# Folds of pairs 1 to 3 on GpSimd alone, and the softmax steps around the experts' first layer put in another order

## The chip, the cores and the metric

One core of a Trainium2 chip, with its engines PE (TensorE), DVE (VectorE), ACT (ScalarE), POOL (GpSimd), SP (SyncE, which only issues DMAs here) and 16 DMA engines. The metric is the device time of one execution in microseconds; several executions are timed, and one more is taken with the hardware profiler.

## The reference

All data are float32. `x` is 8 sequences of 2496 tokens with 256 features.

```python
X = np.fft.fft(np.fft.fft(x, axis=1), axis=2).real      # [8, 2496, 256]
x = X.reshape(19968, 256)
logits = x @ phi                                        # 32 slots = 8 experts x 4
d = softmax(logits, axis=0)                             # over the tokens
slot_input = (d.T @ x).reshape(8, 4, 256)
slot_out[e] = relu(slot_input[e] @ w1[e]) @ w2[e]       # 256 -> 1024 -> 256
out = softmax(logits, axis=1) @ slot_out                # over the slots
```

(Both softmaxes subtract their maximum and add 1e-9 to the sum.)

## The kernel before

The host reorders `x` so that a sequence of 2496 tokens becomes 64 by 39, and the eight sequences become four pairs. The transform is never written out: the logits come from small transforms of `x` times transformed `phi`, and `d.T @ x` is taken on the untransformed side and transformed afterwards. For each pair `p` the kernel loads four pieces `t` of 128x1280 as two DMAs each, `x` and its mirror `xm` (640 KB each, 20.97 MB in all), and then runs these parts, named by one letter in the string `ORDER` (`f13` is part `f` of pair 1, piece 3):

- `f` (line 247) adds `xm` onto `x` in place: the fold. `FOLDV` names the folds on DVE (00 to 03, 13, 23); the others are GpSimd's. A tile of `xm` has five buffers, so the load of a later piece waits for a fold.
- `a` (L253) transposes the folded piece on DVE; `z` (L267) multiplies it with the transformed `phi` on PE into four PSUM banks; `t` (L286) transposes these on DVE. For pair 1, `z12` and `z13` need only pieces 2 and 3; for pair 2 each `z` needs all four pieces.
- `b` (L295) and `c` (L309) finish the logits on PE, ACT copies them out, `n` (L317) takes their maxima on DVE and so frees the banks that the next `z` writes; `i`, `j` turn the maxima round and take the exponential on ACT.
- `e` (L349) and `d` (L367) transform the exponentials back, `u` (L393) multiplies them with the folded `x`: the pair's sum in PSUM. ACT copies the first three pairs' sums to `usb`. `tok` holds the sum of the exponentials.
- `m0` (L430 to L439) rescales between the pairs, `m1` (L442 to L449) adds up `usb` into `acc` and makes the reciprocal from `tok`, `m2` (L451 to L464) adds the last pair's sum and transforms `acc` with small matmuls (accT, slotin) into `sT`.
- `k` issues the loads of the experts' weights into freed buffers. `l` (L475 to L482) is the first layer: 64 matmuls `h`, in two halves of two quarters each; ACT applies the relu to each quarter and DVE transposes it into `hT`. `v` (L490) is the second layer `so`, `r` (L501 to L506) brings its result into `rh`.
- `s`, `S`, `x`, `y`, `g`, `q` are the softmax over the slots, for each pair `p`: transposes of the logits on PE (L517), copies on ACT (L529), and for the two pieces 0 and 1 the maximum on DVE (L538), subtraction on GpSimd (L539), exponential on ACT (L544), sum and reciprocal on DVE (L549 to L551), multiplication on GpSimd (L552) and transposition on DVE (L558).
- `o` (L578, L583, L587) multiplies that with `rh` on PE; ACT and DVE take turns in copying out, and SP issues 23 output DMAs of 20.45 MB in all.
- `W` (L278) is a matmul whose result is not used.

Each engine runs its instructions strictly in the order in which they appear: `in_order` chains each engine's instructions in the order of `LD` (first loads) and `ORDER`. An instruction that waits holds up all that stand behind it on its engine. Loads are issued on SP's queue where the `f` of their piece stands, if `LD` has not issued them.

Of the kernel before, what the change touches and what calls it, by code (L numbers as in the profile page):

```python
# [7 lines left out]
AF = mybir.ActivationFunctionType  # L8
ALU = mybir.AluOpType
# [7 lines left out]
NSLOT = 32  # L17
# [13 lines left out]
LD = "00 0 1 p 01 02 03 2 10 11 3 12 13".split()  # L31

ORDER = (
# [9 lines left out]
).split()  # L43
# [97 lines left out]
def _build(nc, tc, xh, phih, wh, cins, where, out):  # L141
    from contextlib import ExitStack

    v, sc, pe, gp = nc.vector, nc.scalar, nc.tensor, nc.gpsimd
    ctx = ExitStack()
    with ctx:
# [14 lines left out]
        def tagged(shape, name, tag, bufs):  # L161
            return sb.tile(shape, F32, name=name, tag=tag, bufs=bufs)
# [9 lines left out]
        def bank(name):  # L172
            return pp.tile([128, 512], F32, name=name, tag="ps")
# [4 lines left out]
        eo, xm, xT, zb, zt, o1, dpm, esb, dsb = {}, {}, {}, {}, {}, {}, {}, {}, {}  # L178
# [65 lines left out]
        def part_f(p, t):  # L244
            if (p, t) not in eo:
                load_x(p, t)
            (v if f"{p}{t}" in FOLDV else gp).tensor_tensor(eo[p, t], eo[p, t], xm[p, t], op=ALU.add)  # L247

        def part_a(p, t):
            ah, h = t % 2, t // 2  # L250
# [151 lines left out]
        w1t, w2t = [], []  # L402
# [18 lines left out]
        sm = cp.tile([128, 40], F32, name="sm")  # L421
# [5 lines left out]
        def part_m(step):  # L427
            if step == 0:
                ps = bank("msel")
                pe.matmul(  # L430
                    ps[:, : NPAIR * GS], C("sel"), mall.rearrange("p a s -> p (a s)"), start=True, stop=True
                )
                v.tensor_tensor(
                    mm, ps[:, : NPAIR * GS].rearrange("p (a s) -> p a s", s=GS),
                    C("mask").unsqueeze(1).to_broadcast([128, NPAIR, GS]), op=ALU.mult,
                )
                v.tensor_reduce(sm[:, 0:4], mm, axis=AX.X, op=ALU.add)
                v.tensor_reduce(sm[:, 4:5], sm[:, 0:4], axis=AX.X, op=ALU.max, negate=True)
                sc.activation(sm[:, 8:12], sm[:, 0:4], AF.Exp, bias=sm[:, 4:5], scale=1.0)  # L439
                return  # L440
            if step == 1:
                v.tensor_scalar(acc, usb[:, 0], sm[:, 8:9], None, op0=ALU.mult)  # L442
                for p in range(1, NPAIR - 1):
                    v.scalar_tensor_tensor(acc, usb[:, p], sm[:, 8 + p : 9 + p], acc, op0=ALU.mult, op1=ALU.add)
                v.tensor_tensor(sm[:, 12:16], sm[:, 8:12], tok, op=ALU.mult)
                v.tensor_reduce(sm[:, 5:6], sm[:, 12:16], axis=AX.X, op=ALU.add)
                v.tensor_scalar(sm[:, 6:7], sm[:, 5:6], 1e-9, None, op0=ALU.add)
                v.reciprocal(sm[:, 7:8], sm[:, 6:7])
                v.tensor_scalar(sm[:, 16:18], C("mask8"), sm[:, 7:8], None, op0=ALU.mult)  # L449
                return  # L450
            v.scalar_tensor_tensor(acc, ubs[-1][:, :D], sm[:, 11:12], acc, op0=ALU.mult, op1=ALU.add)  # L451
            ps = bank("accT")
            pe.matmul(ps[:, 0:64], acc[:, 0:128], C("psum"), start=True, stop=False)
            pe.matmul(ps[:, 0:64], acc[:, 128:256], C("pdif"), start=False, stop=True)
            pe.matmul(ps[:1, 64:96], acc[:, 0:1], C("psum")[:, 0:32], start=True, stop=False)
            pe.matmul(ps[:1, 64:96], acc[:, 128:129], C("pneg"), start=False, stop=True)
            v.tensor_copy(at[:, :64], ps[:, :64])
            v.tensor_copy(at[:1, 32:64], ps[:1, 64:96])
            for lc in range(2):
                ps = bank3(f"slotin{lc}")  # L460
                ls = slice(lc * 128, lc * 128 + 128)
                pe.matmul(ps[:, :NSLOT], C("ta")[:, ls], at[:, 0:32], start=True, stop=False)
                pe.matmul(ps[:, :NSLOT], C("tb")[:, ls], at[:, 32:64], start=False, stop=True)
                (sc.copy, v.tensor_copy)[lc](sT[:, lc], ps[:, :NSLOT])  # L464
# [2 lines left out]
        rh = []  # L467
        sos_ = []

        def part_l(eh):  # L470
            for fh in range(2):
                ps = bank(f"h{eh}{fh}")
                for lc in range(2):
                    for g in range(4):
                        pe.matmul(  # L475
                            ps[32 * g : 32 * g + 32, :], sT[:, lc, :], w1t[16 * eh + 8 * fh + 4 * lc + g],
                            start=lc == 0, stop=lc == 1, tile_position=(0, 32 * g),
                        )
                hs = tagged([128, 512], f"hs{eh}{fh}", "dpm", 2)
                sc.activation(hs, ps, AF.Relu, scale=sm[:, 16 + eh : 17 + eh])  # L480
                hT[eh, fh] = tagged([128, 16, NSLOT], f"hT{eh}{fh}", "hT", 3)
                v.transpose(hT[eh, fh].rearrange("p f s -> p (f s)"), hs)  # L482

        def part_v(eh):
            if eh == 0:
                sos_.append(pu.tile([128, 512], F32, name="so", tag="u"))
            so = sos_[0]
            for f in range(8):
                for g in range(4):
                    pe.matmul(  # L490
                        so[32 * g : 32 * g + 32, 0:D], hT[eh, f // 4][:, 4 * (f % 4) + g, :],
                        w2t[32 * eh + 4 * f + g],
                        start=eh == 0 and f == 0, stop=eh == 1 and f == 7, tile_position=(0, 32 * g),
                    )
# [102 lines left out]
        def in_order(f, *a):  # L597
# [15 lines left out]
            "f": part_f, "a": part_a, "w": lambda *_: part_w(), "z": part_z, "t": lambda p, _: part_t(p),  # L613
            "b": lambda p, _: part_b(p), "c": part_c, "n": lambda p, _: part_n(p), "i": lambda p, _: part_i(p), "j": lambda p, _: part_j(p),
            "e": part_e, "d": lambda p, _: part_d(p), "u": part_u, "k": lambda i, _: load_w(i),
            "m": lambda i, _: part_m(i), "l": lambda i, _: part_l(i), "v": lambda i, _: part_v(i),
            "r": lambda *_: part_r(), "s": part_s, "S": part_S, "W": part_warm, "x": part_x, "y": part_y, "g": part_g, "q": part_q, "o": part_o,
        }
        for what in LD:
# [59 lines left out]
```

## Time and profile before

| | |
|---|---|
| median of 3 runs | 203.81 us (203.43 to 205.42) |
| the profiled execution's own time | 204.89 us |
| its span, first to last instruction | 202.7 us |
| busy: PE, DVE, ACT, POOL | 158.3, 109.2, 78.5, 50.2 us |
| read and written by DMA | 38.84 MB, 20.45 MB |

The busy shares are means over stages with different limits: loading until about 57 us, dense matmuls until about 121, a chain of small steps until 148.5, output until the end. So the views used below are those in order of time, engine by engine. All times of the trace count from the span's start.

### The profile page before, as it was taken

What the parts mean: (1) busy time and instruction counts of PE and PEld (TensorE: products, weight loads), DVE (VectorE), ACT (ScalarE), POOL (GpSimd) and SP (SyncE); (2) the same over time, 40 slices, a digit from 0 to 9 for tenths busy, and PEclk for the clock granted to TensorE, in tenths of its full rate; (3) what the DMA queues carried; (4) which work ended last, traced back from release to release, by engine and by line L of the source; (5) the groups of instructions that cost most, each with busy time, mean ns of one, the idle gap of its engine ahead of it and who ended that gap; (6) DMA issues with size and microseconds to landing.
All of it is one profiled execution on the core that took longest, in us unless ns stands there. A gap on an engine that the chain in (4) does not pass through costs nothing.

```text
span 202.7 us, 5655 instructions
## 1 busy us (share of the span) xinstructions
PE 158.3 (78%) x2500; PEld 98.3 (48%) x2500; DVE 109.2 (54%) x168; ACT 78.5 (39%) x176; POOL 50.2 (25%) x30
## 2 busy tenths in 40 slices
PE   0496799639989999999999893999889897785000
PEld 0454564339734576457747672624446353563000
DVE  0689286564971592251131076428657999997000
ACT  2001023421650635563647641333048776646000
POOL 0000593999920000000000052314200634400000
PEclk9999999966996999999999997579999999769655
DMA  6999999999910079829967938000019999999995
GB/s 211 401 421 411 405 410 411 415 409 413 413 57 0 5 279 406 348 52 421 428 284 283 384 122 323 7 3 0 3 66 395 415 427 412 420 425 415 423 419 223
DMA packets 11544, 59.65 MB, mean 294 GB/s; under 512 B 1536, under 2 KB 1792, under 8 KB 8448
## 3 DMA queue, kind: packets, MB, share of 16 engines
q1 hardware_dynamic: 11520, 59.29, 72.9%
q8 instruction: 19, 0.31, 0.6%
q14 instruction: 5, 0.04, 0.1%
HBM read 38.84 MB, written 20.45 MB: 292 GB/s over the span
## 4 chain that ended last, share of the span: by engine, by line
PE 41%; DMA 24%; DVE 16%; POOL 5%; issue 3%; ACT 2%; SPq 0%; DVEq 0%; POOLq 0%
DMA xm<-xh 24%; PE u L393 6%; DVE o L583 6%; PE z L267 6%; PE po L578 6%; PE e L349 4%; PE d L367 3%; POOL x L247 3%; PE h L475 3%; PE a L295 3%; PE l L309 3%; DVE cm L549 2%; PE cT L517 2%; POOL c L539 2%; DVE cm L538 2%
## 5 line engine op out<-in xcount | busy, mean ns | idle before, releaser
L247 POOL TENSOR_TENSOR x<-x,xm 128x1280 f32<-128x1280 f32 x10 | 29.8, 2997 | 26.6 <-DMA xm<-xh 26.6
L267 PE MATMUL z<-xT,wz 32*64 32x160 f32 (+1 forms) x768 | 27.6, 388 | 8.3 <-DVE zt L283 6.0
L578 PE MATMUL po<-ct,rh 32*128 32x512 f32 (+1 forms) x192 | 30.1, 615 | 4.3 <-DVE ct L558 1.9
L539 POOL TENSOR_TENSOR c<-c,cm 128x512 f32<-128x512 f32 (+1 forms) x8 | 10.1, 1269 | 84.5 <-DVE cm L538 84.5
L583 DVE COPY o<-po 128x512 f32<-128x512 f32 (+1 forms) x40 | 24.5, 661 | 3.3 <-PE po L578 3.3
L267 PEld LDWEIGHTS z<-xT,wz 32*64 32x64 f32 x768 | 17.5, 148 | 17.0 <-DVE xT L253 6.6
L583 ACT COPY o<-po 128x512 f32<-128x512 f32 (+1 forms) x40 | 21.3, 578 | 9.3 <-PE po L578 8.5
L253 DVE STREAM_TRANSPOSE xT<-x 128x1280 f32<-128x1280 f32 x16 | 23.4, 1492 | 1.8 <-POOL x L247 1.6
L578 PEld LDWEIGHTS po<-ct,rh 32*128 32x128 f32 x192 | 16.8, 205 | 13.4 <-DVE o L583 8.3
L338 ACT ACTIVATE d<-lt,nm 120x128 f32<-120x128 f32 x44 | 13.3, 388 | 19.0 <-DVE zt L283 11.5
L393 PE MATMUL u<-x,ds 128*32 128x256 f32 x320 | 18.6, 380 | 0.0
L286 DVE STREAM_TRANSPOSE zt<-z 128x320 f32<-128x320 f32 x16 | 11.3, 839 | 10.6 <-PE z L267 10.6
L247 DVE TENSOR_TENSOR x<-x,xm 128x1280 f32<-128x1280 f32 x6 | 11.6, 1927 | 9.4 <-DMA xm<-xh 9.4
L552 POOL TENSOR_TENSOR c<-c,cm 128x512 f32<-128x512 f32 (+1 forms) x8 | 10.1, 1263 | 16.2 <-DVE cm L551 12.7
L317 DVE TENSOR_REDUCE mx<-l 120x4 f32<-120x512 f32 (+1 forms) x12 | 7.1, 633 | 12.7 <-ACT lt L312 12.7
L393 PEld LDWEIGHTS u<-x,ds 128*32 128x32 f32 x320 | 11.4, 110 | 4.9 <-issue 0.2
L300 ACT COPY o<-a 128x512 f32<-128x512 f32 (+1 forms) x12 | 6.6, 551 | 17.1 <-PE a L295 16.7
L295 PEld LDWEIGHTS a<-cs,zt 128*64 128x64 f32 x352 | 10.9, 138 | 2.3 <-DVE zt L286 1.0
L295 PE MATMUL a<-cs,zt 128*64 128x64 f32 x352 | 11.7, 223 | 0.3 <-issue 0.2
L349 PE MATMUL e<-cs,d 120*64 120x60 f32 x352 | 11.5, 225 | 0.3 <-issue 0.3
L349 PEld LDWEIGHTS e<-cs,d 120*64 120x64 f32 x352 | 10.9, 140 | 1.0 <-issue 0.8
L355 ACT COPY e<-e 128x480 f32<-128x480 f32 (+1 forms) x12 | 6.4, 530 | 12.5 <-PE e L349 12.1
(87 smaller groups left out, 165.8 us busy)
## 6 DMA issues: line engine op xcount, KB each, us to landing
out<-o SPq DMA_DIRECT2D x15, 1024.0 KB, 9.1
w<-wh SPq DMA_DIRECT2D x9, 1280.0 KB, 7.3
x<-xh SPq DMA_DIRECT2D x16, 640.0 KB, 11.2
xm<-xh SPq DMA_DIRECT2D x16, 640.0 KB, 10.6
out<-o SPq DMA_DIRECT2D x4, 896.0 KB, 10.3
w<-wh SPq DMA_DIRECT2D x5, 512.0 KB, 10.5
out<-o SPq DMA_DIRECT2D x4, 256.0 KB, 3.1
w<-wh SPq DMA_DIRECT2D x1, 896.0 KB, 7.4
```

The lines of the kernel that those rows point to most:

```text
L247: (v if f"{p}{t}" in FOLDV else gp).tensor_tensor(eo[p, t], eo[p, t], xm[p, t], op=ALU.add)
L253: v.transpose(xT[p, ah][:, XW * h : XW * h + XW], eo[p, t])
L267: pe.matmul(zb[p][i][64 * ah : 64 * ah + 64, 160 * h0 : 160 * (h0 + n)], wz[r, j % 4, j // 4, :], xv[r, :, j, :], start=j == 0, stop=j == ...
L286: v.transpose(o[:, :, NQ * i : NQ * i + NQ], zb[p][i][:, :320].rearrange("p (h q s) -> p h q s", h=2, s=32))
L295: pe.matmul(ps[64 * r : 64 * r + 64, 64 * i : 64 * i + 64], zt[p][:, o : o + 64], C("wa")[:, 64 * r : 64 * r + 64], start=True, stop=True, ...
L338: sc.activation(d[:, g], lt[p][:, g0 + g], AF.Exp, bias=nm[:, g0 + g : g0 + g + 1], scale=1.0)
L349: pe.matmul(o[64 * k : 64 * k + 64, :, h, g], dd[p, b][:, g, 64 * h : 64 * h + 64], C("ec")[:, 60 * k : 60 * k + 60].rearrange("p (c x) -> ...
L393: pe.matmul(ub[32 * g : 32 * g + 32, 0:D], dsb[p][:, k, h, ah, q, :], eo[p, 2 * h + ah][:, D * q : D * q + D], start=cc == 0, stop=cc == 9 ...
L539: gp.tensor_tensor(c, c, m[:, 0].unsqueeze(2).to_broadcast([128, n, NSLOT]), op=ALU.subtract)
L552: gp.tensor_tensor(c, c, m[:, 1].unsqueeze(2).to_broadcast([128, n, NSLOT]), op=ALU.mult)
L578: pe.matmul(po[:, j * w : j * w + w], rh[0][rows, 128 * dc : 128 * dc + 128], t[rows, r0 * NSLOT : r0 * NSLOT + w], start=True, stop=True, ...
L583: (v.tensor_copy if n_ev[0] % 2 else sc.copy)(ot[:, o : o + w * len(dcs)], po[:, : w * len(dcs)])
```

## The change

Folds 13 and 23 go to GpSimd, and `f13` and `f23` stand in `ORDER` with the others of their pairs, which also moves their loads. The matmul `W31` goes; `a23` stands behind `n10`. `m1` is cut in two: `m1` (the sums over `usb`) stands right behind `m0`, `m2` (from `tok` to the reciprocal) before pair 0's softmax, and what was `m2` is `m3`. `l` is issued by quarters, with `hT` in four buffers, and the softmax steps of pairs 0 and 1 stand between them in another order.

```diff
--- before.py
+++ after.py
@@ -23,7 +23,6 @@
 ZW = 664
 RING, NXM, NET = 8, 5, 2
 
-FOLDV = ("00", "01", "02", "03", "13", "23")
 APART = (0, 1)
 KP = ((0, 16), (16, 24))
 CT = ["sa", "lt", "lt", "lt"]
@@ -31,13 +30,13 @@
 LD = "00 0 1 p 01 02 03 2 10 11 3 12 13".split()
 
 ORDER = (
-    "f00 a00 w00 f01 a01 z00 z01 f02 a02 f03 a03 z02 z03 W23 f10 f11 f12 f20 f21 f22 f30 f31 f32 f33 "
-    "t00 a10 a11 b00 c00 c01 a12 c02 n00 z10 z11 i00 j00 W31 f13 a13 z12 z13 "
-    "e00 e01 e02 t10 b10 a20 a21 d00 a22 c10 c11 c12 f23 a23 n10 "
+    "f00 a00 w00 f01 a01 z00 z01 f02 a02 f03 a03 z02 z03 W23 f10 f11 f12 f13 f20 f21 f22 f23 f30 f31 f32 f33 "
+    "t00 a10 a11 b00 c00 c01 a12 c02 n00 z10 z11 i00 j00 a13 z12 z13 "
+    "e00 e01 e02 t10 b10 a20 a21 d00 a22 c10 c11 c12 n10 a23 "
     "z20 z21 i10 z22 j10 z23 t20 u00 u01 k00 k10 b20 a30 a31 a32 a33 e10 e11 e12 c20 c21 c22 n20 d10 "
     "z30 z31 i20 z32 j20 z33 k20 t30 u10 u11 k30 b30 k40 e20 e21 e22 c30 c31 c32 n30 d20 "
-    "i30 u20 j30 u21 k50 m00 s00 s01 s02 e30 e31 e32 k60 d30 S00 S01 S02 x00 x01 y00 y01 u30 m10 g00 u31 s10 m20 k70 s11 s12 "
-    "S10 S11 S12 g01 x10 l00 q00 x11 y10 y11 q01 g10 g11 l10 q10 q11 v00 v10 r00 "
+    "i30 u20 j30 u21 k50 m00 m10 s00 s01 s02 e30 e31 e32 k60 d30 u30 m20 S00 S01 S02 x00 x01 y00 u31 s10 m30 k70 s11 s12 "
+    "y01 g00 g01 S10 S11 S12 x10 x11 l00 l01 y10 q00 q01 l10 y11 g10 l11 g11 v00 q10 q11 v10 r00 "
     "o00 s20 S20 o01 s21 S21 o02 s22 S22 o03 x20 x21 o04 y20 o10 y21 g20 o11 g21 s30 S30 o12 q20 s31 S31 o13 s32 S32 x30 o14 q21 x31 "
     "o20 y30 o21 y31 g30 o22 g31 o23 q30 o24 q31 o30 o31 o32 o33 o34"
 ).split()
@@ -244,7 +243,7 @@
         def part_f(p, t):
             if (p, t) not in eo:
                 load_x(p, t)
-            (v if f"{p}{t}" in FOLDV else gp).tensor_tensor(eo[p, t], eo[p, t], xm[p, t], op=ALU.add)
+            (v if p == 0 else gp).tensor_tensor(eo[p, t], eo[p, t], xm[p, t], op=ALU.add)
 
         def part_a(p, t):
             ah, h = t % 2, t // 2
@@ -442,6 +441,8 @@
                 v.tensor_scalar(acc, usb[:, 0], sm[:, 8:9], None, op0=ALU.mult)
                 for p in range(1, NPAIR - 1):
                     v.scalar_tensor_tensor(acc, usb[:, p], sm[:, 8 + p : 9 + p], acc, op0=ALU.mult, op1=ALU.add)
+                return
+            if step == 2:
                 v.tensor_tensor(sm[:, 12:16], sm[:, 8:12], tok, op=ALU.mult)
                 v.tensor_reduce(sm[:, 5:6], sm[:, 12:16], axis=AX.X, op=ALU.add)
                 v.tensor_scalar(sm[:, 6:7], sm[:, 5:6], 1e-9, None, op0=ALU.add)
@@ -467,19 +468,18 @@
         rh = []
         sos_ = []
 
-        def part_l(eh):
-            for fh in range(2):
-                ps = bank(f"h{eh}{fh}")
-                for lc in range(2):
-                    for g in range(4):
-                        pe.matmul(
-                            ps[32 * g : 32 * g + 32, :], sT[:, lc, :], w1t[16 * eh + 8 * fh + 4 * lc + g],
-                            start=lc == 0, stop=lc == 1, tile_position=(0, 32 * g),
-                        )
-                hs = tagged([128, 512], f"hs{eh}{fh}", "dpm", 2)
-                sc.activation(hs, ps, AF.Relu, scale=sm[:, 16 + eh : 17 + eh])
-                hT[eh, fh] = tagged([128, 16, NSLOT], f"hT{eh}{fh}", "hT", 3)
-                v.transpose(hT[eh, fh].rearrange("p f s -> p (f s)"), hs)
+        def part_l(eh, fh):
+            ps = bank(f"h{eh}{fh}")
+            for lc in range(2):
+                for g in range(4):
+                    pe.matmul(
+                        ps[32 * g : 32 * g + 32, :], sT[:, lc, :], w1t[16 * eh + 8 * fh + 4 * lc + g],
+                        start=lc == 0, stop=lc == 1, tile_position=(0, 32 * g),
+                    )
+            hs = tagged([128, 512], f"hs{eh}{fh}", "dpm", 2)
+            sc.activation(hs, ps, AF.Relu, scale=sm[:, 16 + eh : 17 + eh])
+            hT[eh, fh] = tagged([128, 16, NSLOT], f"hT{eh}{fh}", "hT", 4)
+            v.transpose(hT[eh, fh].rearrange("p f s -> p (f s)"), hs)
 
         def part_v(eh):
             if eh == 0:
@@ -613,7 +613,7 @@
             "f": part_f, "a": part_a, "w": lambda *_: part_w(), "z": part_z, "t": lambda p, _: part_t(p),
             "b": lambda p, _: part_b(p), "c": part_c, "n": lambda p, _: part_n(p), "i": lambda p, _: part_i(p), "j": lambda p, _: part_j(p),
             "e": part_e, "d": lambda p, _: part_d(p), "u": part_u, "k": lambda i, _: load_w(i),
-            "m": lambda i, _: part_m(i), "l": lambda i, _: part_l(i), "v": lambda i, _: part_v(i),
+            "m": lambda i, _: part_m(i), "l": part_l, "v": lambda i, _: part_v(i),
             "r": lambda *_: part_r(), "s": part_s, "S": part_S, "W": part_warm, "x": part_x, "y": part_y, "g": part_g, "q": part_q, "o": part_o,
         }
         for what in LD:
```

GpSimd's queue of folds before (`x_0_99`, `x_1_103` are pair 1's `x`, `x_0_288`, `x_1_293` pair 2's, the number behind `xm_` is the piece, the last row is of pair 3):

```order
L247 TENSOR_TENSOR x_0_99<-x_0_99,xm_2_108 128x1280 [waits DMAHW2_49,DMAHW1_49]
L247 TENSOR_TENSOR x_0_288<-x_0_288,xm_0_289 128x1280 [waits DMAHW6_49,DMAHW5_49]
L247 TENSOR_TENSOR x_1_293<-x_1_293,xm_1_294 128x1280 [waits DMAHW7_49,DMAHW0_49]
L247 TENSOR_TENSOR x_0_288<-x_0_288,xm_2_298 128x1280 [waits DMAHW2_49,DMAHW1_49]
L247 TENSOR_TENSOR x_0_302<-x_0_302,xm_0_303 128x1280 [waits DMAHW4_49,DMAHW3_49]
```

and with the change (`x_0_289`, `x_1_294` are now pair 2's):

```order
L246 TENSOR_TENSOR x_0_99<-x_0_99,xm_2_108 128x1280 [waits DMAHW2_49,DMAHW1_49]
L246 TENSOR_TENSOR x_1_103<-x_1_103,xm_3_111 128x1280 [waits DMAHW4_49,DMAHW3_49]
L246 TENSOR_TENSOR x_0_289<-x_0_289,xm_0_290 128x1280 [waits DMAHW6_49,DMAHW5_49]
L246 TENSOR_TENSOR x_1_294<-x_1_294,xm_1_295 128x1280 [waits DMAHW7_49,DMAHW0_49]
L246 TENSOR_TENSOR x_0_289<-x_0_289,xm_2_299 128x1280 [waits DMAHW2_49,DMAHW1_49]
L246 TENSOR_TENSOR x_1_294<-x_1_294,xm_3_303 128x1280 [waits DMAHW4_49,DMAHW3_49]
```

Fold 13 stands between 12 and 20, fold 23 between 22 and 30; the loads moved with fold 23, so that the last piece to come in is 33 instead of 23.

DVE's queue before, from pair 2's transposes to its maxima (`xT` is the transposed piece, `mx` the maxima of pair 1's logits):

```order
L253 STREAM_TRANSPOSE xT_0_662<-x_0_288 128x1280 [waits Pool_49]
L247 TENSOR_TENSOR x_1_293<-x_1_293,xm_3_702 128x1280 [waits DMAHW4_49,DMAHW3_49]
L253 STREAM_TRANSPOSE xT_1_664<-x_1_293 128x1280 [waits DVE_49]
L317 TENSOR_REDUCE mx_707<-l_0_693 120x4 [waits Activation_49]
L317 TENSOR_REDUCE mx_707<-l_1_696 120x4 [waits Activation_49]
L317 TENSOR_REDUCE mx_707<-l_2_699 120x3 [waits Activation_49]
```

and with the change:

```order
L252 STREAM_TRANSPOSE xT_0_664<-x_0_289 128x1280 [waits Pool_49]
L316 TENSOR_REDUCE mx_704<-l_0_695 120x4 [waits Activation_49]
L316 TENSOR_REDUCE mx_704<-l_1_698 120x4 [waits Activation_49]
L316 TENSOR_REDUCE mx_704<-l_2_701 120x3 [waits Activation_49]
L252 STREAM_TRANSPOSE xT_1_666<-x_1_294 128x1280 [waits Pool_49]
```

The fold has left the queue, and the last transpose stands behind the maxima.

DVE's queue before, between pair 0's softmax maxima (`cm`) and the last pair's sum (`u`):

```order
L538 TENSOR_REDUCE cm_1_1508<-c_1405 128x24
L442 TENSOR_SCALAR acc<-usb,sm 128x256
L444 SCALAR_TENSOR_TENSOR acc<-usb,sm,acc 128x256 [waits DVE_49] x2
L445 TENSOR_TENSOR sm<-sm,tok 128x4 [waits Activation_49]
L446 TENSOR_REDUCE sm<-sm 128x1 [waits DVE_49]
L447 TENSOR_SCALAR sm<-sm 128x1 [waits DVE_49]
L448 RECIPROCAL sm<-sm 128x1 [waits DVE_49]
L449 TENSOR_SCALAR sm<-cs_70,sm 128x2 [waits DVE_49]
L549 TENSOR_REDUCE cm_0_1505<-c_1405 128x16
L550 TENSOR_SCALAR cm_0_1505<-cm_0_1505 128x16 [waits DVE_49]
L551 RECIPROCAL cm_0_1505<-cm_0_1505 128x16 [waits DVE_49]
L451 SCALAR_TENSOR_TENSOR acc<-u_1523,sm,acc 128x256 [waits PE_49]
```

and with the change:

```order
L450 TENSOR_SCALAR sm<-cs_70,sm 128x2 [waits DVE_49]
L538 TENSOR_REDUCE cm_0_1542<-c_1406 128x16 [waits Activation_49]
L538 TENSOR_REDUCE cm_1_1545<-c_1406 128x24
L452 SCALAR_TENSOR_TENSOR acc<-u_1513,sm,acc 128x256 [waits PE_49]
L458 COPY at<-accT 128x64 [waits PE_49]
L459 COPY at<-accT 1x32 [waits DVE_49]
L465 COPY sT<-slotin_1587 128x32 [waits PE_49]
L549 TENSOR_REDUCE cm_0_1542<-c_1406 128x16 [waits Activation_49]
```

Only the two maxima stand between the small steps on `sm` and the last pair's sum; the softmax's sums and reciprocals come behind the copy of `sT`.

## Rows read from the trace of the kernel before

**Rows 1.** The page's second part, the span in 40 slices of 5.07 us: TensorE's granted clock in tenths, and what the DMA engines moved.

```profile
PEclk9999999966996999999999997579999999769655
...
GB/s 211 401 421 411 405 410 411 415 409 413 413 57 0 5 279 406 348 52 421 428 284 283 384 122 323 7 3 0 3 66 395 415 427 412 420 425 415 423 419 223
```

**Rows 2.** The chain that ended last, in order of time, between 28 and 59 us: start us, us, what.

```profile
28.41 12.79 DMA xm<-xh
...
47.99 8.99 DMA xm<-xh
...
57.08 1.50 DVE x L247
```

**Rows 3.** SyncE's queue in order of time, from 126 us on: start us, us, engine, line, operation.

```profile
150.32 36.82 SPq L587 DMA_DIRECT2D out<-o  x23
```

**Rows 4.** DVE in order of time, 36 to 62 us: start us, us, engine, line, operation, in brackets the idle time before and what ended it.

```profile
38.17 0.17 DVE L334 COPY nm<-mt 120x11 f32<-120x11 f32 x1 [0.32 <-PE mt L332]
...
38.26 4.10 DVE L247 TENSOR_TENSOR x<-x,xm 128x1280 f32<-128x1280 f32 x1
...
42.40 1.51 DVE L253 STREAM_TRANSPOSE xT<-x 128x1280 f32<-128x1280 f32 x1
...
48.52 2.83 DVE L286 STREAM_TRANSPOSE zt<-z 128x320 f32<-128x320 f32 x4 [4.55 <-PE z L267]
...
60.04 1.72 DVE L317 TENSOR_REDUCE mx<-l 120x4 f32<-120x512 f32 x3
```

**Rows 5.** The view of line 247 (the fold), its GpSimd and its DVE instructions: count, shortest/median/longest ns, first and last start, form.

```profile
L247 POOL TENSOR_TENSOR x<-x,xm x10: 2883/2914/3782, 20.9 to 54.0; 128x1280 f32<-128x1280 f32 x10
...
L247 DVE TENSOR_TENSOR x<-x,xm x6: 1491/1493/4102, 6.7 to 57.1; 128x1280 f32<-128x1280 f32 x6
```

**Rows 6.** PE in order of time, 22 to 88 us, columns as in Rows 4.

```profile
22.94 1.33 PE L267 MATMUL z<-xT,wz 32*64 32x160 f32 x60 [1.27 <-issue]
...
38.06 1.13 PE L278 MATMUL warm<-cs,cs 128*128 128x512 f32 x2
...
43.96 4.54 PE L267 MATMUL z<-xT,wz 32*64 32x160 f32 x120 [4.34 <-DVE zt L283]
...
51.41 0.33 PE L295 MATMUL a<-cs,zt 128*64 128x64 f32 x2
...
56.85 2.62 PE L309 MATMUL l<-o,cs 128*120 128x512 f32 x6
...
83.84 2.41 PE L267 MATMUL z<-xT,wz 32*64 32x320 f32 x64
```

**Rows 7.** Busy time of each engine in stretches of the front: us, busy us and instructions of PE, PE's weight loads, DVE, ACT, POOL, then the granted clock, the DMA share and GB/s.

```profile
40.00:44.00 4.00, 0.04 (x6) 0.04 (x6) 3.94 (x3) 1.76 (x7) 3.68 (x2) 0.76 1.01 408
...
44.00:48.50 4.50, 4.50 (x122) 4.04 (x123) 0.00 (x0) 0.00 (x0) 4.50 (x3) 0.50 1.02 415
...
48.50:51.50 3.00, 3.00 (x90) 2.89 (x91) 2.98 (x5) 1.15 (x3) 3.00 (x2) 0.93 1.01 407
...
60.00:65.00 5.00, 4.41 (x63) 2.37 (x62) 1.75 (x4) 0.00 (x0) 0.00 (x0) 0.76 0.01 2
```

**Rows 8.** GpSimd in order of time, 20 to 62 us, columns as in Rows 4.

```profile
28.48 2.91 POOL L247 TENSOR_TENSOR x<-x,xm 128x1280 f32<-128x1280 f32 x1 [0.37 <-DMA xm<-xh]
...
34.86 2.89 POOL L247 TENSOR_TENSOR x<-x,xm 128x1280 f32<-128x1280 f32 x1 [3.47 <-DMA xm<-xh]
...
41.33 12.39 POOL L247 TENSOR_TENSOR x<-x,xm 128x1280 f32<-128x1280 f32 x4 [0.32 <-DMA xm<-xh]
...
53.97 2.94 POOL L247 TENSOR_TENSOR x<-x,xm 128x1280 f32<-128x1280 f32 x1 [0.25 <-DMA xm<-xh]
```

**Rows 9.** One later pair's row maxima: DVE, then the matmuls of PE that they follow, 99 to 103 us, columns as in Rows 4.

```profile
101.55 1.16 DVE L317 TENSOR_REDUCE mx<-l 120x4 f32<-120x512 f32 x2 [0.17 <-ACT lt L312]
...
99.44 2.10 PE L309 MATMUL l<-o,cs 128*120 128x512 f32 x5
```

**Rows 10.** PE in order of time, 116 to 149 us, columns as in Rows 4.

```profile
116.11 4.82 PE L393 MATMUL u<-x,ds 128*32 128x256 f32 x79
...
124.80 0.66 PE L453 MATMUL accT<-cs,acc 128*128 128x64 f32 x2 [3.31 <-DVE acc L451]
...
129.80 9.27 PE L475 MATMUL h<-w,sT 128*32 128x512 f32 x64
...
143.17 3.66 PE L490 MATMUL so<-w,hT 128*32 128x256 f32 x64 [0.65 <-DVE hT L482]
...
148.55 1.14 PE L578 MATMUL po<-ct,rh 32*128 32x512 f32 x8 [0.52 <-DVE rh L506]
```

**Rows 11.** DVE in order of time, 119 to 125 us, columns as in Rows 4.

```profile
119.99 2.10 DVE L444 SCALAR_TENSOR_TENSOR acc<-usb,sm,acc 128x256 f32<-128x256 f32 x2
...
122.25 0.17 DVE L445 TENSOR_TENSOR sm<-sm,tok 128x4 f32<-128x4 f32 x1 [0.15 <-ACT tok L386]
...
124.26 0.39 DVE L451 SCALAR_TENSOR_TENSOR acc<-u,sm,acc 128x256 f32<-128x256 f32 x1
```

**Rows 12.** GpSimd in order of time at the same place, columns as in Rows 4.

```profile
118.76 2.54 POOL L539 TENSOR_TENSOR c<-c,cm 128x512 f32<-128x512 f32 x2 [61.85 <-DVE cm L538]
```

**Rows 13.** The first layer of the experts in two stretches, columns as in Rows 7.

```profile
129.87:134.20 4.33, 4.33 (x24) 1.05 (x28) 0.87 (x2) 1.11 (x2) 2.48 (x2) 0.50 0.01 4
...
134.70:139.00 4.30, 4.30 (x48) 1.21 (x44) 2.81 (x5) 1.21 (x2) 0.35 (x1) 1.00 0.00 0
```


## The prediction

> **What bounds the kernel now.** I read the slices first, to see where DMA is the limit and where not. It moves over 400 GB/s in slices 2 to 11 (5 to 56 us) and again from slice 31 on; between, most of all from 127 to 147 us, it moves next to nothing [rows 1]. So loading and storing are two stretches of fixed length, and what lies between decides. The last piece of `x` lands at 47.99 + 8.99 = 56.98 us, and the chain runs through these loads into a fold on DVE [rows 2]. The first output is issued at 150.32 [rows 3] and DMA is full from then to the end of the span, so the end follows the first output at a fixed distance: 202.7 less the start of `po` at 148.55 [rows 10] is 54.2 us. Everything gained ahead of `po` is gained at the end.
>
> In the middle I then read each engine in order of time and look for holes of PE. **Front:** PE stands idle 4.34 us ahead of 43.96 [rows 6], because fold 13 on DVE takes 4.10 us (38.26 to 42.36) [rows 4] where the median DVE fold takes 1.49 [rows 5]; its transpose ends at 43.91. The granted clock then is 0.50 (1.2 of 2.4 GHz) from 44 to 48.5 [rows 7], so 120 `z` matmuls take 4.54 us [rows 6] instead of 2 x 1.33 = 2.66, at the full rate of the 60 at 22.94 [rows 6]. A second hole follows `c12`, which ends at 56.85 + 2.62 = 59.47 [rows 6]: `z20` writes into banks that pair 1's maxima free, and these, behind fold 23 and its transpose, end at 60.04 + 1.72 = 61.76 [rows 4]. From there to the end of `u31` at 116.11 + 4.82 = 120.93 [rows 10] PE has no such hole. **Tail:** accT starts at 124.80 after 3.31 us of idle [rows 10], since the last sum on DVE starts only at 124.26, behind steps that wait for `tok` until 122.25 [rows 11]. After that hole the clock is at 0.50 as far as 134.20 [rows 13].
>
> **Front, with the change.** GpSimd gets two folds more: 12 x 2.91 = 35.0 us [rows 5]. A piece of `x` is 1.31 MB, 3.19 us at 411 GB/s [rows 1]; twelve are 38.3 us, so GpSimd keeps up. Fold 13 falls into the 3.47 us that GpSimd now idles ahead of 34.86 [rows 8] and is over by about 34.5. Loads wait for folds no later than before. Fold 23 takes the place of the second of the four folds from 41.33 [rows 8] and ends near 47.5; fold 33 becomes the last, 57 to 60 us, and pair 3's `z` starts only at 83.84 [rows 6], so I cost it at nothing.
>
> On DVE the transpose `a13` follows the copy that ends at 38.34 [rows 4]: 38.35 to 39.87 with 1.51 us [rows 4]. The rest of `z12`, `z13` runs from 39.9 for 2.6 us to 42.5 (before: 48.50): 4.1 us from the fold, 1.9 from the clock. The warm matmul of 1.13 us [rows 6] goes, which costs nothing as PE waits there. `t10` takes 2.83 us [rows 4], to 45.4; `b10` started then too (51.35, 51.41), and from there to the end of `c12` took 59.47 - 51.41 = 8.06 [rows 4, 6]: now 53.5. The maxima of a pair end 102.71 - 101.54 = 1.17 us after its last `l` matmul [rows 9], at 54.7, and `a23`, now behind them, adds 1.51: `z20` runs on at 56.2, against 61.76. **Front: 5.6 us.** What is late next is that wait of 2.7 us, 0.4 longer than before; I let the clock fall there as it did (0.76 on the mean from 60 to 65) [rows 7].
>
> Ends: if the clock falls already at `z12`, the 1.9 and some 0.4 in `e` are lost: 3.3. If it doesn't fall at `z20` either, the 62 matmuls there gain 2.4 more by the 64 at 83.84 [rows 6]: 8.0.
>
> **Tail, with the change.** The sums over `usb` move to where DVE is idle, and there GpSimd is idle too; the 2.10 us of line 444 [rows 11] lie beside two subtractions on GpSimd that run to 121.30 [rows 12], but nothing waits there any more. `tok`'s copy goes ahead of pair 0's copies on ACT (about 0.15 us, hidden under `u`), and the five small steps under `u` as well. The last sum starts with `u`'s end at 120.95, takes 0.39 [rows 11], and accT starts where PE's idle time now begins, 124.80 - 3.31 = 121.5 [rows 10]: 3.3 us earlier, with no hole. From accT to the first layer took 129.80 - 124.80 = 5.0 us, nearly all at half clock; at full clock the PE part of some 4.6 halves, so it lies between 2.7 and 5.0. I take 4.2, since these matmuls are small and the clock may fall among them: the layer starts at 125.7.
>
> The 64 `h` take 9.27 us, 24 in 4.33 at half and 48 in 4.30 at full clock [rows 10, 13]. All at full clock would be 5.7. I take 8.2, a half-clock stretch a little shorter than now, since there is still some low work before it: end 133.9 instead of 139.07. The second half of `so` now waits 0.65 us for `hT` [rows 10]. That wait ends 4.1 us after the last `h` (143.17 - 139.07), with both late quarters' steps ahead of it; now the first of them is done while PE works at the last, so 133.9 + 4.1 = 138.0 is the latest, when `v00`, 3.66 long like the half in the row, ends at 137.6. So I let the 0.65 go: `so` ends at 141.2 instead of 146.83, and with 0.1 off for it **tail: 5.5 us.** GpSimd's work of pair 0 and 1 (2.54 for two subtractions [rows 12]) and the exponential `y01`, moved behind `sT`, end before it; they are costed at nothing. If that cover goes, they hold `v10` or the first output.
>
> Ends: 3.3, if only accT's start moves; 9.8 (3.3 + 2.3 + 3.5 + 0.65) if the clock stays full, of which I hold 1.3 back, since the softmax steps ahead of `hT` on DVE and GpSimd then have that much less time: 8.5.
>
> **The sum.** 5.6 + 5.5 = 11.1 us. The profiled execution took 204.89 us, so it would take 193.8; it stands 1.08 above the median of 203.81, by which the forecast is **192.7 us**.
>
> **The rivals.** *The clock falls at the wait ahead of `z12`.* For it: a shorter wait, at 59.5 to 61.8, was followed by half clock too [rows 7], and the warm matmul is gone. The tail holds: 203.8 - 3.3 - 5.5 = 195.0. The Trainium skill's page "TensorE: Matmul & The Clock Gate" (Why this matters for your kernels) speaks for this rival: it wants no idle gaps between bursts of matmuls, as the clock drops back after one. The trace agrees at 44 us (0.50) [rows 7].
>
> *The tail gives back what follows accT*, with half clock as long as now or `hT` late behind the softmax: 203.8 - 5.6 - 3.3 = 194.9; both rivals together 197.2. *The tail stays at full clock*: 203.8 - 5.6 - 8.5 = 189.7.
>
> *GpSimd's slower folds reach the path.* It folds in 2.91 us where DVE's median is 1.49 [rows 5]; two folds more would cost 2 x 1.42 = 2.8: 195.5. Against: both have slack, 38.35 - 34.5 and 54.7 - 47.5, and on DVE fold 13 took 4.10 [rows 4]. "GPSIMD Engine Reference" of the Trainium skill (4.1 Engine selection) is the rule against this change: it keeps elementwise work on VectorE, GpSimd being about half as fast. The ratio agrees here; the 4.10 shows that its advice would not pay beside busy GpSimd.
>
> *Slower than before:* the clock falls at `z12` and stays down until `c12` ends. The 2.66 us of `z` and 59.47 - 48.50 = 11.0 us behind it double: `z20` at 69.8 instead of 61.76, 8.0 lost; less 5.5 it gives 206.3. It decides from 11.1 us of such work on. Against: after the fall at 44 the clock was back at 0.93 on the mean from 48.5 to 51.5, with PE dense [rows 7]. *No change* would need outputs or loads as the bound through the middle, and DMA is idle for 20 us ahead of the first output [rows 1].
>
> **How the numbers follow.** Forecast (190.9 to 194.6) 0.48; full clock in the tail 0.14; tail given back 0.14; clock at `z12` 0.12; both 0.05; GpSimd 0.03; no change 0.02; slower 0.02. From 189.0, a little under the fast case, to 197.5, just above the two losses together, leaves out about 0.1 by these cases; the sizes of the clock's stretches are the least certain, so I keep that. About 1% is what a measurement tells from no change: faster 0.95, same 0.03, slower 0.02.
>
> **What would show it.** GpSimd: 12 folds of 2.9 us, the last near 60. DVE: `a13` at 38.4, no fold after 19 us. PE: `z` running on at about 40 and 56, accT right behind `u`, at about 116 (121.5 - 5.6); first `po` near 137.5 and DMA full from there to the end, 54 us. Wrong it would be if PE's clock is at half for long behind `z12`, if `so` waits for `hT`, if GpSimd's folds run late and loads pause before 57 us, or if the end does not follow `po`.

## The result, and the profile after

The changed kernel takes **193.91 us** (median of four runs, 193.27 to 194.54) against 203.62 us for the kernel before on the same chip: a ratio of 0.951 (0.944 to 0.957), 9.7 us less. The profiled execution took 193.27 us, span 191.0.

The page of the changed kernel: the granted clock and the DMA rate by slice (4.78 us each), and the group of the folds, with its busy us, mean ns and idle time:

```profile
PEclk9999759997999999999999999999999999759755
...
GB/s 196 409 413 411 405 410 417 411 409 417 407 334 5 7 206 411 411 81 274 424 415 162 411 281 227 239 3 3 0 302 419 424 424 410 422 424 415 425 418 206
...
L246 POOL TENSOR_TENSOR x<-x,xm 128x1280 f32<-128x1280 f32 x12 | 34.8, 2904 | 24.7 <-DMA xm<-xh 24.7
```

Against [rows 1], the clock has lost both of its lows in the middle, the one at the end of the front and the one ahead of the experts; a dip at 43 us is left. One at 22 us, at 0.50 from 21.8 to 28.6 us, is new here but not the change's: traces of the old front have one there too (that of experiment 5 from 21.0 to 24.5), and experiment 6, with the new front, has none. The twelve folds take as long as forecast. DMA loads for as long as before, and the first output is issued at 138.54 instead of 150.32 us [rows 3].

PE of the changed kernel in order of time, in the front (start us, us, engine, line, operation, in brackets the idle time before and what ended it):

```profile
41.43 3.94 PE L266 MATMUL z<-xT,wz 32*64 32x160 f32 x120 [1.25 <-DVE xT L252]
45.30 2.94 PE L348 MATMUL e<-cs,d 120*64 120x60 f32 x88
48.09 0.34 PE L294 MATMUL a<-cs,zt 128*64 128x64 f32 x4
49.81 2.67 PE L294 MATMUL a<-cs,zt 128*64 128x64 f32 x84 [1.38 <-issue]
...
54.72 2.62 PE L308 MATMUL l<-o,cs 128*120 128x512 f32 x6
57.27 2.04 PE L266 MATMUL z<-xT,wz 32*64 32x320 f32 x8
59.98 2.38 PE L266 MATMUL z<-xT,wz 32*64 32x320 f32 x56 [0.67 <-DVE xT L252]
```

and DVE at the same places, with the sums over `usb` and the last sum further on:

```profile
39.88 1.50 DVE L252 STREAM_TRANSPOSE xT<-x 128x1280 f32<-128x1280 f32 x1
...
45.21 2.83 DVE L285 STREAM_TRANSPOSE zt<-z 128x320 f32<-128x320 f32 x4 [3.77 <-PE z L266]
...
58.42 1.50 DVE L252 STREAM_TRANSPOSE xT<-x 128x1280 f32<-128x1280 f32 x1
...
107.94 1.00 DVE L443 SCALAR_TENSOR_TENSOR acc<-usb,sm,acc 128x256 f32<-128x256 f32 x2
...
117.53 0.48 DVE L452 SCALAR_TENSOR_TENSOR acc<-u,sm,acc 128x256 f32<-128x256 f32 x1 [1.18 <-PE u L392]
```

The hole of 4.34 us [rows 6] is 1.25, and the fold is gone from DVE. But `z` takes 3.94 us, and inside `b10`, after four of its 88 records (the views show two for one matmul), PE stops for 1.38 us with nothing to wait for that the profile shows ("issue"). In the kernel before, the same stop was 0.16:

```profile
51.90 2.72 PE L295 MATMUL a<-cs,zt 128*64 128x64 f32 x86 [0.16 <-issue]
...
60.74 4.92 PE L267 MATMUL z<-xT,wz 32*64 32x320 f32 x62 [0.59 <-DVE mx L317]
```

So `z20` runs on at 59.98 instead of 61.76, where the maxima ahead of it end [rows 4]: only 1.8 earlier.

The granted clock, by stretches (columns as in Rows 7):

```profile
42.40:45.70 3.30, 3.30 (x88) 2.85 (x79) 0.49 (x1) 0.98 (x4) 3.06 (x2) 0.50 1.03 417
45.70:48.00 2.30, 2.30 (x84) 2.30 (x83) 2.30 (x5) 0.97 (x2) 2.04 (x2) 1.00 1.00 403
...
60.00:65.00 5.00, 5.00 (x122) 2.64 (x122) 0.76 (x4) 0.72 (x3) 0.00 (x0) 1.00 0.01 3
121.08:127.97 6.89, 6.89 (x66) 2.10 (x68) 5.64 (x12) 4.25 (x8) 5.02 (x4) 1.00 0.18 72
```

From 60 to 65 it is 1.00 where it was 0.76 [rows 7]: with that, `u31` ends 3.4 us earlier, at 117.49 instead of 120.93 [rows 10]. But this fall is not in every execution of the old front. Experiments 2, 3 and 5 have that front, and their traces show 1.00 there; experiment 4's shows 0.75. The row of experiment 5:

```profile
60.00:65.00 5.00, 4.62 (x81) 2.27 (x87) 2.28 (x6) 0.39 (x1) 0.00 (x0) 1.00 0.01 2
```

So the 3.4 us hold some luck of the two executions: `u31` ends between 118.97 and 120.93 in the five traces with the old front, and at 117.49 and 116.35 (experiment 1) in the two with the front as changed. In the changed kernel the clock is 1.00 in the first layer too. PE at the tail:

```profile
112.91 4.58 PE L392 MATMUL u<-x,ds 128*32 128x256 f32 x80
...
118.16 0.41 PE L454 MATMUL accT<-cs,acc 128*128 128x64 f32 x2
...
121.08 7.07 PE L475 MATMUL h<-w,sT 128*32 128x512 f32 x64
127.97 7.09 PE L490 MATMUL so<-w,hT 128*32 128x256 f32 x128
...
136.77 0.71 PE L578 MATMUL po<-ct,rh 32*128 32x512 f32 x4 [0.52 <-DVE rh L506]
```

From `u`'s end to `po` it took 148.55 - 120.93 = 27.6 us [rows 10]; now 136.77 - 117.49 = 19.3, which is 8.3 less, and it is 19.3 in every trace with the changed tail. Front and tail give 11.8, the whole difference in `po` (148.55 to 136.77), and from `po` to the end of the span it is 191.0 - 136.8 = 54.2 us, as before. Against the medians' 9.7 that is 2 more; the profiled execution of before was a slow one, by 1.08 us against its median on record.

### The profile page after: what moved, and what is told of

It is laid out like the page before. It is cut to its first block, busy times and chain, and to the rows that moved or that the text cites. A ratio compares the mean times of both kernels' runs of the same rounds, so it can differ in the third digit from the quotient of the medians.

```text
span 191.0 us, 5651 instructions
## 1 busy us (share of the span) xinstructions
PE 153.1 (80%) x2498; PEld 95.8 (50%) x2498; DVE 103.0 (54%) x166; ACT 78.2 (41%) x176; POOL 55.2 (29%) x32
## 4 chain that ended last, share of the span: by engine, by line
PE 62%; DVE 16%; DMA 8%; issue 4%; ACT 1%; SPq 0%; DVEq 0%
PE z L266 11%; PE u L392 9%; DMA xm<-xh 8%; DVE o L583 7%; PE po L578 6%; PE a L294 6%; PE e L348 6%; PE d L366 5%; PE l L308 5%; PE h L475 4%; PE so L490 4%; PE warm L277 2%; DVE xT L252 2%; PE cT L517 2%; DVE cm L549 2%
## 5 line engine op out<-in xcount | busy, mean ns | idle before, releaser
L246 POOL TENSOR_TENSOR x<-x,xm 128x1280 f32<-128x1280 f32 x12 | 34.8, 2904 | 24.7 <-DMA xm<-xh 24.7
L578 PE MATMUL po<-ct,rh 32*128 32x512 f32 (+1 forms) x192 | 31.0, 607 | 4.5 <-DVE ct L558 2.1
L266 PE MATMUL z<-xT,wz 32*64 32x160 f32 (+1 forms) x768 | 26.3, 376 | 5.3 <-DVE xT L252 3.4
L266 PEld LDWEIGHTS z<-xT,wz 32*64 32x64 f32 x768 | 17.0, 145 | 12.7 <-DVE xT L252 4.5
L308 PE MATMUL l<-o,cs 128*120 128x512 f32 (+1 forms) x24 | 10.5, 573 | 0.0
L246 DVE TENSOR_TENSOR x<-x,xm 128x1280 f32<-128x1280 f32 x4 | 6.0, 1492 | 7.5 <-DMA xm<-xh 7.5
```

Of the source, the lines that this page charges most:

```text
L246: (v if p == 0 else gp).tensor_tensor(eo[p, t], eo[p, t], xm[p, t], op=ALU.add)
L266: pe.matmul(zb[p][i][64 * ah : 64 * ah + 64, 160 * h0 : 160 * (h0 + n)], wz[r, j % 4, j // 4, :], xv[r, :, j, :], start=j == 0, stop=j == ...
L308: pe.matmul(ps[:120, : 128 * n], C("wc"), o1[p][:, g0 : g0 + n].rearrange("p g k -> p (g k)"), start=True, stop=True)
L578: pe.matmul(po[:, j * w : j * w + w], rh[0][rows, 128 * dc : 128 * dc + 128], t[rows, r0 * NSLOT : r0 * NSLOT + w], start=True, stop=True, ...
```

## The experiments

Each run is compared with the kernel before on the same chip.

**1. The front alone** (folds, their loads, no `W31`, `a23` behind `n10`).

```diff
-FOLDV = ("00", "01", "02", "03", "13", "23")
-... f10 f11 f12 f20 f21 f22 f30 ... j00 W31 f13 a13 z12 z13 ... c12 f23 a23 n10
+... f10 f11 f12 f13 f20 f21 f22 f23 f30 ... j00 a13 z12 z13 ... c12 n10 a23
```

> Only the front of the change: all folds of pairs 1 to 3 on GpSimd, loads in their order, no warm matmul ahead of z12, a23 behind n10; the tail as before. Split as forecast (front 5.6, tail 5.5): 203.6 - 5.6 = 198.0 us. Split as the one profile of the change reads (end of u31 117.49 against 120.93 before): 203.6 - 3.4 = 200.2. If the folds on GpSimd gave nothing and all came from the tail: 203.6.

Measured: 200.59 us against 202.75, ratio 0.985 (0.976 to 0.994): 2.2 us. In its trace the tail is the old one, PE in order of time:

```profile
120.48 0.66 PE L452 MATMUL accT<-cs,acc 128*128 128x64 f32 x2 [3.57 <-DVE acc L450]
...
125.48 9.24 PE L474 MATMUL h<-w,sT 128*32 128x512 f32 x64
```

By the medians the front alone is worth less than half of the 5.6 us forecast for it; the interval of the ratio leaves 1.3 to 4.9.

**2. The tail alone** (the changed kernel with the four places of experiment 1 put back).

> Only the tail of the change: sums over pairs and tok ahead, quarters of the first layer; folds and loads as before. Split as forecast: 203.6 - 5.5 = 198.1 us. Split as the profile of the change reads (u31's end to the first po 19.28 against 27.62 us): 203.6 - 8.3 = 195.3, with the granted clock at 1.00 from accT to the end of the second layer.

Measured: 195.18 us, ratio 0.958 (0.951 to 0.966): 7.6 us. With experiment 1 that is 9.7, the whole change: the parts add up. PE of this kernel:

```profile
120.28 0.41 PE L454 MATMUL accT<-cs,acc 128*128 128x64 f32 x2
...
123.19 7.07 PE L475 MATMUL h<-w,sT 128*32 128x512 f32 x64
130.08 7.09 PE L490 MATMUL so<-w,hT 128*32 128x256 f32 x128
```

**3 and 4. The two halves of the tail.** The sums alone (`m1` cut in two and moved, first layer by halves as before), and the quarters with their order alone (`m` as before):

```diff
-k50 m00 s00 ... d30 S00 S01 S02 x00 x01 y00 y01 u30 m10 g00 u31 s10 m20 k70 ... S12 g01 x10
+k50 m00 m10 s00 ... d30 u30 m20 S00 S01 S02 x00 x01 y00 y01 u31 s10 m30 k70 ... g00 ... S12 g01 x10
```

```diff
-S10 S11 S12 g01 x10 l00 q00 x11 y10 y11 q01 g10 g11 l10 q10 q11 v00 v10 r00
+g01 S10 S11 S12 x10 x11 l00 l01 y10 q00 q01 l10 y11 g10 l11 g11 v00 q10 q11 v10 r00
```

> Only the sums over pairs, the last token's copy and the small steps on sm moved under e and u; the first layer in halves and the softmax steps as before, but for pair 0's first sum behind s12. Theory that the clock carries the tail: without the 3.3 us hole ahead of accT the clock stays at 1.00, accT to h shrinks by about 2.1 and h by 2.2, with 3.3 for the start 7.6: 196.0 us. Theory that the order alone counts: 3.3, 200.3, with the clock at 0.50 among accT and h as before.

> Only the quarters of the first layer with the softmax steps between them; sums over pairs as before, so the 3.3 us hole ahead of accT stays. Theory that the clock carries the tail: h is at 0.50 as before and only the wait of so for hT (0.65 us) goes: 202.9 us. Theory that the quarters carry it: 4 to 5 us, 199, with so starting that much earlier.

Measured: sums 196.93 us, ratio 0.967 (0.958 to 0.975), 5.8 us; quarters 203.8, ratio 1.002 (0.998 to 1.007), nothing. PE with the sums alone, and then with the quarters alone:

```profile
123.44 7.07 PE L477 MATMUL h<-w,sT 128*32 128x512 f32 x64
...
134.60 3.66 PE L492 MATMUL so<-w,hT 128*32 128x256 f32 x64 [0.64 <-DVE hT L484]
```

```profile
124.81 0.66 PE L453 MATMUL accT<-cs,acc 128*128 128x64 f32 x2 [3.50 <-DVE acc L451]
...
129.81 9.23 PE L474 MATMUL h<-w,sT 128*32 128x512 f32 x64
138.87 7.08 PE L489 MATMUL so<-w,hT 128*32 128x256 f32 x128
```

The sums close the hole, and the clock stays up by itself; the wait of `so` for `hT` is then still there (0.64). The quarters remove that wait, and `po` comes 0.87 earlier in that trace (147.68), but in the medians it doesn't show. On top of the sums, `u`'s end to `po` goes from 20.13 to 19.29 us with them, 0.84 by the traces of experiments 3 and 2. Their medians lie 1.75 apart, but the intervals of the two ratios overlap.

**5. The clock by itself.** The kernel before, with three unused matmuls put into the hole ahead of accT: nothing else is moved.

> The kernel before, with nothing moved: three matmuls of 128x512 whose result is not used are put on PE into the hole ahead of accT (about 2.8 us of it). If the clock carries the tail: accT still starts 3.3 us after the four transposes, but the granted clock stays at 1.00, accT to h shrinks from 5.0 to about 2.9 us and the 64 h from 9.3 to 7.1: 4.3 us, 202.8 - 4.3 = 198.5. If only the order of the steps counts: 202.8.

Measured: 198.93 us against 202.97, ratio 0.983 (0.977 to 0.988): 4.0 us, from useless work alone. PE:

```profile
119.37 2.75 PE L283 MATMUL fill<-w,cs 128*128 128x512 f32 x6
123.10 0.41 PE L458 MATMUL accT<-cs,acc 128*128 128x64 f32 x2 [0.98 <-DVE acc L456]
...
126.01 7.07 PE L480 MATMUL h<-w,sT 128*32 128x512 f32 x64
```

accT starts 4.1 us after `u`, no sooner than before (3.9), but accT to `h` takes 2.9 instead of 5.0 and `h` 7.07 instead of 9.27 [rows 10]: 4.3 us. So about half of the tail's gain is the clock, and half the work moved out of the hole. The Trainium skill's page "TensorE: Matmul & The Clock Gate" (Why this matters for your kernels), which asks for no idle gaps between bursts, agrees here.

**6. `a23` ahead of `n10`** in the changed kernel: its place before, without the fold.

```diff
-c10 c11 c12 n10 a23
+c10 c11 c12 a23 n10
```

> The change, with a23 ahead of n10 on DVE again. Fold 23 ends on GpSimd at 47.4, long before its turn, so a23 is off the path: z20 runs on with the end of the maxima, 1.5 us earlier: 193.9 - 1.5 = 192.4. If z20 is held by something else (the clock falling behind the shorter wait, or the fold after all): 193.9 or more.

Measured: 191.86 us, ratio 0.946 (0.941 to 0.951), the lowest of all. By the medians it is 2 us under the changed kernel, by the ratios 1.0, and their intervals overlap. DVE, then PE:

```profile
46.73 5.67 DVE L252 STREAM_TRANSPOSE xT<-x 128x1280 f32<-128x1280 f32 x4
```

```profile
48.22 2.67 PE L294 MATMUL a<-cs,zt 128*64 128x64 f32 x84 [0.93 <-issue]
...
53.12 2.62 PE L308 MATMUL l<-o,cs 128*120 128x512 f32 x6
55.68 3.68 PE L266 MATMUL z<-xT,wz 32*64 32x320 f32 x64
```

Once fold 23 is done in time, `a23` fits beside `b10` and `d00`, and `z20` follows `c12` without the 2.6 us of wait. It still follows the maxima there and runs more slowly than at full speed: the 64 records of `z20` and `z21` end 3.6 us after `c12` (59.36 - 55.74) instead of 5.0 (62.36 - 57.34). That is 1.4 us gained, near the 1.5 expected. Most of the rest of this trace's lead comes from `a13`, which starts 1.4 us earlier without the dip at 22 us.

**7 and 10. `W31` put back**, to keep the clock up at `z12`: in the changed kernel, and in the one of experiment 6.

> The change, with the warm matmul W31 kept ahead of z12. If taking it away let the clock fall in z12 and z13 (3.9 us for 120 matmuls in the two profiles, 2.66 at full clock): 1.2 us less, 192.7. If the clock falls there anyway, as it did behind W31 in the kernel before: 193.9.

> e6_a23_first with the warm matmul W31 kept. From e7_warm: z12, z13 at full clock end 1.2 us earlier, but b10 then stops the longer (2.5 us in that profile), so nothing comes of it: 191.9. If the full clock is worth what it saves: 190.7.

Measured: 193.01 us, ratio 0.951 (0.946 to 0.956), and 193.3, ratio 0.947 (0.940 to 0.955): no gain on either. PE of experiment 7:

```profile
41.66 1.84 PE L266 MATMUL z<-xT,wz 32*64 32x160 f32 x83 [0.19 <-DVE xT L252]
43.75 1.03 PE L266 MATMUL z<-xT,wz 32*64 32x160 f32 x37 [0.25 <-issue]
...
50.40 2.73 PE L294 MATMUL a<-cs,zt 128*64 128x64 f32 x86 [2.54 <-issue]
```

`z` is at full speed, 3.1 us instead of 3.94. But the stop in `b10` grows to 2.54, and comes after two of its records instead of four: `W31` is two records. It stands at a fixed number of instructions, and one packet of 0.02 MB of the queue "q8 instruction" goes with each stop. This one runs from 47.99 to 49.06 us, and PE goes on at 50.40. In every trace with a stop in `b10`, PE goes on 1.3 to 1.5 us after such a packet's end. The two stops in the rows are 37 + 88 + 2 = 127 matmul records apart, with their weight loads 254 instructions. The page "Runtime: NRT & Kernel Launch" (Instruction fetch mechanics) of the Trainium skill says that instructions come in blocks of 256; the trace agrees to within two. It adds that the cost is mostly hidden; here it isn't, with 2.54 us.

**8. Fold 13 on DVE again**, everything else as changed.

> The change, with fold 13 alone back on DVE at its old place, loads in the order of the change. If a DVE fold waits until the fold that GpSimd is at has ended: it starts at 39 to 40 and ends 1.5 us after GpSimd's fold 21, near 42.5, a13 ends near 44 instead of 41.4: 2.6 us more, 196.5. If it runs beside GpSimd in its 1.49 us: 41.4, a13 at 42.9: 1.5 us more, 195.4. If the folds' engine makes no difference here: 193.9.

Measured: 195.13 us, ratio 0.962 (0.957 to 0.967), 1.2 us slower than the changed kernel by the medians, 2.2 by the ratios; the two intervals just touch at 0.957. In the traces `po` comes 2.9 us later (139.70). DVE, GpSimd and PE:

```profile
38.94 3.86 DVE L246 TENSOR_TENSOR x<-x,xm 128x1280 f32<-128x1280 f32 x1
```

```profile
38.57 2.89 POOL L246 TENSOR_TENSOR x<-x,xm 128x1280 f32<-128x1280 f32 x1 [0.20 <-DMA xm<-xh]
```

```profile
44.40 4.54 PE L266 MATMUL z<-xT,wz 32*64 32x160 f32 x120 [5.16 <-DVE xT L252]
...
52.14 2.99 PE L294 MATMUL a<-cs,zt 128*64 128x64 f32 x88
```

DVE's fold ends at 42.80, 1.34 us after GpSimd's (41.46), which is about an undisturbed fold's own 1.49 [rows 5]; it took 4.10 [rows 4] in the same position. In the five traces with the old front, fold 13 ends 1.35 us after GpSimd's, and the GpSimd fold behind it takes 3.8 us instead of 2.9 [rows 5]. The Trainium skill's "SBUF — State Buffer" (SBUF: two separate sides) tells of a port pair that whichever of the two begins holds for its whole instruction; the trace agrees. And `b10`, which starts 4.05 us later than in the changed kernel (52.14 to 48.09), runs without a stop and ends 55.13 to 52.48: 1.4 of the 4.05 had gone into the stop.

**9. The stop moved.** The kernel of experiment 6 with 42 unused one-column matmuls (84 records) ahead of `z12`.

> The change with a23 ahead of n10 (e6_a23_first) and 42 matmuls of one column, 84 records on PE, put into the wait ahead of z12; their result is not used. In six profiles PE stops for 0.2 to 2.5 us inside b10, after its 4th matmul without W31 and after its 2nd with it, which adds two; an instruction load of 0.02 MB comes 2.3 to 2.7 us ahead of its going on. If the stop belongs to a place in PE's stream of instructions (128 matmuls apart: the one before lies after the 83rd of z12, z13), it moves by 84 records, to the start of z12 and into e: none is left in b10, and with PE busy in the wait z12 may run at full clock: 191.9 - 0.9 = 191.0, down to 190. If it belongs to b10 and what it waits for: the stop stays after its 4th matmul and the time at 191.9.

Measured: 197.82 us against 203.31, ratio 0.974 (0.968 to 0.980): 6 us slower than experiment 6. PE, and then the clock (columns as in Rows 7):

```profile
38.30 3.51 PE L282 MATMUL tiny<-cs,cs 128*32 128x1 f32 x84
41.74 4.97 PE L266 MATMUL z<-xT,wz 32*64 32x160 f32 x128
46.64 0.56 PE L353 MATMUL e<-cs,d 120*64 120x60 f32 x9
48.29 2.49 PE L353 MATMUL e<-cs,d 120*64 120x60 f32 x78 [1.09 <-issue]
...
54.43 1.39 PE L299 MATMUL a<-cs,zt 128*64 128x64 f32 x40 [2.19 <-issue]
...
98.39 0.92 PE L353 MATMUL e<-cs,d 120*64 120x60 f32 x24 [2.12 <-issue]
```

```profile
40.00:46.80 6.80, 6.80 (x167) 6.19 (x165) 0.49 (x2) 2.00 (x7) 6.02 (x3) 0.50 1.01 409
```

The stop went where the count puts it: from the 5th record of `b10` to the 10th of the 88 of `e` ahead of it (83 records earlier, for 84 added). So it belongs to a place in PE's stream of instructions. But this didn't take it off the path. In experiment 6 the next block's end comes only behind the long matmuls of `d` and `c` (84 + 32 + 6 records from 48.22 on); here it falls into `b10` too and stops 2.19 us, and another one 2.12 at 96 us, where experiment 6 has one of 0.99 at 72 us. The full clock that was hoped for did not come either: PE was busy through the wait with the added matmuls, and the clock was at 0.50 from 40.0 to 46.8 all the same. Of the 6.0 us by which `po` comes later (140.28, in experiment 6 134.28), `z20` has 60.61 - 55.68 = 4.9: 1.7 since the added matmuls hold `z` up (41.74 to 40.05), 1.0 since `z` is longer at half clock, the rest from the stops. That I had not foreseen.

## Why the prediction was right, and where its steps were not

The sum was near: 11.1 us against 11.6 by the profiled executions (204.89 to 193.27) and 9.7 by the medians, and 192.7 us against 193.91. **Its split was not**: forecast were 5.6 for the front and 5.5 for the tail; the traces gave 3.4 and 8.3, the medians of experiments 1 and 2 2.2 and 7.6. Two errors of opposite sign met, and that the sum held is luck. What happened is two of the rivals at once, the clock falling at `z12` and the tail at full clock. By the prediction's own prices that is 203.8 - 3.3 - 8.5 = 192.0, a case that it did not list.

**Front.** Right: GpSimd keeps up (last fold 57.05 to 59.94), the DVE fold's 4.10 goes, nothing waits longer for loads, and the wait ahead of `z20` is 2.64 (57.34 to 59.98) where 2.7 was said. `z20` should have run on at 56.2; it did at 59.98, 3.8 later. `a13` started 1.5 late, at 39.88, which is this execution's: the clock was at 0.50 from 21.8 to 28.6 us; in experiment 6 `a13` starts at 38.49. The other terms were mis-sized. "The rest of `z12`, `z13` ... for 2.6 us" took 3.94: the rival of the clock at `z12`, given 0.12, is what happened, though only to 45.7 us. And "from there to the end of `c12` took 8.06" became 9.25, since the stop in `b10`, 0.16 before, grew to 1.38: the instructions of that place don't come sooner because PE is there sooner. This step I did not have at all. On the other side, "I let the clock fall there as it did" was wrong: at `z20` it stayed at 1.00 in the changed kernel and gave back 1.5 by the trace. It stays there in all seven traces with the new front, whole or with one place altered (the change, experiments 1 and 6 to 10), but also in three of the five with the old front, so these 1.5 us are not the change's for certain.

**Tail.** accT 3.3 us earlier against `u`: 3.2 measured (3.87 us after `u`'s end, now 0.67), right. No wait of `so`: right. The size of the clock's part was wrong: accT to `h` 4.2 forecast and 2.9 measured, `h` 8.2 forecast and 7.07 measured. The clock did not fall in the small matmuls from accT to `h`, once the hole ahead of them was gone; I had held on to half clock for much of that stretch "since there is still some low work before it". The case "The tail stays at full clock" (8.5) came out, at 8.3, where I had given it 0.14. Its own sum was 9.8 less 1.3 held back, with `h` at 5.7 us. That was misread: `h` at full clock is 7.07. The two stretches of [rows 13] count 24 + 48 = 72 of the 64 records, as each also counts those that its edges cut; the second holds about 40, which would have given 6.9. The 1.3 held back for another reason made up for it.

**Rivals.** "The tail gives back" fell with experiment 2. "GpSimd's slower folds reach the path": no, `a13` waited for no fold, and experiment 8 shows DVE's fold 13 as the worse one. "Slower than before": no, the clock was at 1.00 again from 45.7 on. Of the signs, these came true: `po` at 136.77 (forecast 137.5), 54.2 us to the end, no fold on DVE after 19 us, the last fold near 60. Those of the front's gain did not: `a13` at 39.88 (38.4), `z` at 41.43 and 59.98 (40 and 56), accT at 118.16 (116).

**Open.** The medians hold 9.7 of the 11.8 by the two traces; the rest is how single executions differ (the clock's falls of before are not in the same places in each run), and I did not separate it further. Fold 23 and the order of the loads were not taken by themselves. What sets the moment at which an instruction block is asked for was not tried.

## What to carry to other kernels

Look for PE's hole first and for the clock after it: a hole ahead of a dense stage costs itself and then the half clock of what follows, about as much again here. Work that doesn't need the last result goes ahead of that point on its own engine; cutting what comes behind it showed nothing in the medians while the hole was there (experiment 4). Useless work in a hole does not always help: the three matmuls of 128x512 in experiment 5 were followed by a clock of 1.00, the 42 of one column in experiment 9 by 0.50. And where a stage starts earlier, look for "issue" stops in the short matmuls that follow it. Look also for folds on DVE that run beside GpSimd's.

## What the runs showed of the hardware

- PE stops at fixed numbers of instructions, about 128 matmul records and their weight loads apart, when these run through before the next block is there: 0.16 to 2.54 us each in `e` and `b10`, and PE goes on 1.3 to 1.5 us after the end of an instruction packet. In experiments 7 and 9 a block's first matmul came 6.65 us (43.75 to 50.40) and 6.14 us (48.29 to 54.43) after that of the block before, both with short matmuls and the loads of `x` at over 400 GB/s. In the changed kernel the packets start at 40.98, 47.25 and 53.42 during these loads, and at 57.14 as they end. That the loads slow the packets is not shown. A warm-up that made PE faster there gained nothing.
- Three unused matmuls in a hole of 3.3 us, ahead of small matmuls and then a dense stage, brought 4.0 us.
- A DVE add of two tiles in SBUF (128x1280) that starts beside a GpSimd add of the same kind ends 1.34 to 1.35 us after GpSimd's in six traces, whether it starts 0.14 us behind that one's start (38.26 and 38.12, the kernel before) or 1.60 (40.33 and 38.73, experiment 2).
